# A recurrent-memory transformer block on one core: first rows ahead of the weights, one more key projection in the opening, one more feed-forward pair inside the recurrence

## The chip, the cores and the metric

The kernel runs on one core of a Trainium2 chip. The metric is the device time of one execution in microseconds (us); lower is better. The core has five engines with their own instruction streams: TensorE (PE) for matmuls, VectorE (DVE), ScalarE (ACT), GpSimd (POOL) and SyncE (SP), which only issues DMAs here. Each engine works through its own list in order.

## The reference

Two layers follow each other: attention over segments with a recurrent memory, then a gated feed-forward layer. Cut to what matters:

```python
# x: 2048 x 640, 32 heads of 128, segments of 32 tokens, memory of 8 rows
n_seg = 64; mem = mem0
for s in range(n_seg):
    h = concat([mem, LN(x)[32*s:32*s+32]])          # 40 rows
    q, k, v = h @ Wq, h @ Wk, h @ Wv                # 640 -> 32 heads x 128
    scores = q @ k.T * scale                        # per head, 40 x 40
    scores = where(mask, scores, -1e9)              # memory columns always, the rest causal
    o = (softmax(scores) @ v) @ Wo                  # 4096 -> 640
    mem = o[:8]; outs.append(o[8:])
h = x + concat(outs)
gate, up = LN(h) @ W_gate, LN(h) @ W_up             # 640 -> 1728
out = h + (relu(gate) * up) @ W_down                # 1728 -> 640
```

The memory makes the 64 segments a chain: segment s + 1 needs the first eight output rows of segment s.

## The kernel before

**Order of the work.** Every instruction is added to one list by hand (`add`), and `_Graph.solve` derives the waits from the keys that each names as read (`r`) or written (`w`). Within an engine the order of adding is the order of execution, so an instruction that waits holds up all that is behind it on its engine. A DMA that reads a tile holds the tile's next writer until it has landed. Most DMAs are issued by SP.

**Rows of a segment.** A segment has 40 rows: eight memory rows, 24 further rows ("early" tokens) and eight last ones ("late" tokens, `RID` = 24 to 31). A projection for a segment takes 32 columns at a time: memory and early tokens of that segment in `act_r`, and the late tokens of four segments together in `act_e`. `project` computes one of Wk, Wq, Wv (`j` = 1, 0, 2) for such a set of 32 rows: five chunks of the contraction, two halves of the heads, four matmuls of 128x512 side by side in column groups of 32, 40 matmuls in all.

**Opening.** The three attention weights come in 15 chunks of 1 MB in the order keys, queries, values, then Wo in eight pieces, all through SP. Meanwhile the first row sets are normalised (`row_stats`, `row_scale`, `ln1_trans`, `ln1_back`) and projected as each chunk lands (`opening`). `unit(n, j, ...)` projects the late tokens of later segments (`LATER[n]`), which need nothing of the memory: n = 0, 1, 2 are the groups of segments 58 to 61, 54 to 57 and 50 to 53. `keep` puts the keys and queries found into tiles that are idle in the opening (`HOMES`), and `spill` saves them to DRAM (`next_d`) when the opening is over. `warm` issues filler matmuls on a zeroed tile. The opening ends when segment 0's output has gone through Wo; its last product (`wo_pass`, L616) needs the last piece of Wo. Behind `spill` in SP's list come saves of the values in `Vp` (`lastv_d`), of `tok` 2 and 3 (`farv_d`) and of `ends`.

**Steps.** The loop `for s in range(1, 64)` runs a step per segment, some 12 us each: keys, queries and values of segment s, scores, softmax, values, Wo, and the memory for s + 1 (`to_act_split`). In step 1 the first half of the queries goes to `tok` 2. In the stretch where the recurrence leaves TensorE nothing to do, a step has an extra unit (`extra_units`): in the steps s % 4 = 2, 3, 0 the keys, queries and values of the late tokens of the next four segments; in s % 4 = 1 the Wo product of late tokens. In steps s of `EARLY` and the three after each, one block of 128 rows is finished, normalised and turned for the feed-forward layer (`xn2_d`). `fill_of` says how many projection matmuls of a step are cut into two halves of 256 columns.

**Pairs ahead of time.** Late tokens of the last segments have been projected in the opening, so the extra unit of steps 46 to 48, 50 to 52, 54 to 56 and 58 to 60 (`EARLY_STEPS`) is free and holds `early_product`: one pair (gate and up, 128 columns of the 1728) of the feed-forward layer for a block of 512 rows. Its rows and weights are fetched in the step before (`early_rows`, `early_weights`), its result goes to `hx_d`. There are nine pairs of block 0 (`NE`) and three of block 1 (`NX`).

**Feed-forward.** After the last segment come blocks 0 to 3 of 512 rows: 13 pairs and a tail each (`gate_up`, L1095 and L1108) less what was done ahead, then the down products (`down_pair`, L1434 and L1449). Block 1 loads the pairs done ahead from `hx_d` into `hT[1]`.

Of the kernel before, what the change touches and what calls it, by code (L numbers as in the profile page):

```python
# [177 lines left out]
def build_kernel(nc, A_x, A_mem0, A_Wq, A_Wk, A_Wv, A_Wo, A_seg_len, B_W_gate, B_W_up, B_W_down, out):  # L178
# [23 lines left out]
    NE = 9  # L202
    NX = 3
    next_d = [nc.dram_tensor(f"next{i}_d", [128, 32 * H], BF16) for i in range(6)]
# [73 lines left out]
    rs = ar.alloc("rs", [128, 1], F32)  # L278
    ps = es.enter_context(nc.psum_tensor("ps", [128, 4096], F32))
# [26 lines left out]
    add("pool", lambda p: p.memset(wtok[:], 0.0), w=[("wtok",)])  # L306
# [51 lines left out]
    def row_moments(src, skey, n, more=()):  # L358
        for q in range(2):
            add("dve", lambda v, q=q: v.bn_stats(st[0:n, q, :], src[0:n, q * 320:(q + 1) * 320]), r=[skey, *more],  # L360
                w=[("st", q)])
        add("dve", lambda v: v.bn_aggr(mv[0:n, :], st[0:n, :, :]), r=[("st", 0), ("st", 1)], w=[("mv",)])

    def row_std(n):
        add("act", lambda a: a.activation(lv[0:n, :], mv[0:n, 1:2], ACTF.Ln, bias=eps[0:n, 0:1], scale=1.0),
            r=[("mv",), ("eps",)], w=[("lv",)])
        add("act", lambda a: a.activation(rs[0:n, :], lv[0:n, :], ACTF.Exp, scale=-0.5), r=[("lv",)], w=[("rs",)])
# [5 lines left out]
    def row_scale(src, skey, n, dst, dkey, eng="dve"):  # L373
        add(eng, lambda v: v.tensor_scalar(dst[0:n, :], src[0:n, :], mv[0:n, 0:1], rs[0:n, 0:1], ALU.subtract,
                                             ALU.mult), r=[skey, ("mv",), ("rs",)], w=[dkey])
# [73 lines left out]
    HEAD = 64 + SEG + M  # L449
# [8 lines left out]
    def ln1_back(b, src, r, eng, kinds=(0, 1)):  # L458

        n = n_rows(b)  # L460

        def copy(dst, sl, w):
            if eng == "pool":
                add("pool", lambda p: p.tensor_copy(dst, sl), r=r, w=w)
            else:
                add("dve", lambda v: v.tensor_copy(dst, sl), r=r, w=w)
        if b < 0:
            copy(act_r[1][:, 0:2, :, M:32], src[:, :, 0:2 * SEG].rearrange("p c (e t) -> p e c t", t=SEG)[:, :, :, 0:RID],
                 [("act", 1, "x", e) for e in range(2)])
            for e, t0 in ((0, RID), (2, 2 * SEG)):  # L470
# [303 lines left out]
    def mem_load(g, eng):  # L774
        dma(wtok[32 * g:32 * g + M, :, :],
            mem0_ap.rearrange("t (c g j) -> g t c j", g=4, j=32)[g], r=[("wtok",)], w=[("wtok0", g)], eng=eng)

    for g in range(3):
        mem_load(g, "act")
    srcs = (A_Wq, A_Wk, A_Wv)  # L780
    for j in (1, 0, 2):
        for c in range(DC):
            dma(W[:, j, c, :], srcs[j][128 * c:128 * c + 128].rearrange("p h e -> p (h e)"), w=[("W", j, c)])
            if j == 1 and c == 0:
                mem_load(3, "sp")
            if j == 1 and c == 1:
                dma(xl[0:LATE, :], x_ap[SEG * (NSEG - 14):SEG * (NSEG - 2), :].rearrange("(e t) d -> e t d", t=SEG)[:, RID:SEG, :],
                    w=[("xl",)])
# [15 lines left out]

    warm(20)
    ln1_trans(-1, xt, ("xt",), P0)
    ln1_back(-1, chunks_of(bank_bf(P0)[:, 0:D]), [B(P0)], "dve")
# [6 lines left out]
    LATER = tuple((act_r[1][:, 4 - n], [("act", 1, 4 - n, "m"), ("act", 1, "x", 4 - n), ("act", 1, "x")]) for n in (1, 2)) + (  # L814
        (xl[:, 0:DC * 32].rearrange("p (c t) -> p c t", t=32), [("xl",)]),)
# [12 lines left out]
    opening(1, 0, (0, 1))  # L828
    warm(6)
    row_stats(x0, ("oTe", 0), 128)  # L830
    row_scale(x0, ("oTe", 0), 128, x0, ("oTe", 0))
    ln1_trans(0, x0, ("oTe", 0), P1)
    ln1_back(0, chunks_of(bank_bf(P1)[:, 0:D]), [B(P1)], "dve", (1,))
    opening(1, 0, (2,))
    warm(2)
    row_stats(xl, ("xl",), LATE)
    w0 = bank(P0)[:, 0:160]
    copy_op("dve", w0, wtok[:].rearrange("p c t -> p (c t)"), [("wtok",)] + [("wtok0", g) for g in range(4)],
            [B(P0), ("w0",)])
    to_act(0, ("w0",), w0)  # L840
    row_scale(xl, ("xl",), LATE, xl, ("xl",))
    ln1_back(0, chunks_of(bank_bf(P1)[:, 0:D]), [B(P1)], "dve", (0,))
    opening(1, 1, range(3))
    opening(1, 0, (3,))
    opening(1, 1, (3,))
    opening(1, 2, range(4))
# [3 lines left out]
            late_rows[:, :, 32:96].rearrange("p c (e t) -> p c e t", t=32), [B(P0)], LATER[0][1][:2] + LATER[1][1][:2])  # L850
    copy_op("dve", LATER[2][0], late_rows[:, :, 0:32], [B(P0)], [("xl",)])
# [3 lines left out]
    def turn(j, n, t):  # L855
        for i in range(2):
# [3 lines left out]
            else:  # L860
# [5 lines left out]
    HOMES = {(0, 1): [(Ve[0], 512 * i, VE_KEYS) for i in range(2)], (0, 0): [(oTe, 512 * i, oTe_keys) for i in range(2)],  # L866
             (1, 1): [(oT[1], 512 * i, OT_KEYS) for i in range(2)], (1, 0): [(at, 0, [("at",)]), (xt, 0, [("xt",)])],
             (2, 1): [(Ko, 512 * i, [("Ko", i) for i in range(2)]) for i in range(2)],
             (2, 0): [(Qo, 512 * i, QO_KEYS) for i in range(2)]}

    def keep(n, j, banks, t):
        for i in range(2):
            home, off, ks = HOMES[n, j][i]
            to_tok(banks[i], t + i, "act")
            add("dve", lambda v, home=home, off=off, i=i: v.transpose(ap(home, off, [[1, 512]]), tok[t + i][:, :]),
                r=tok_keys(t + i), w=ks)

    def spill(n, j):
        parts = HOMES[n, j]
        k = 2 * n + 1 - j  # L880
        if parts[0][0] is parts[1][0]:
            dma(next_d[k][:, :], ap(parts[0][0], 0, [[1, 32 * H]]), r=parts[0][2], w=[("next", k)])
            return
        for i, (home, off, ks) in enumerate(parts):
            dma(next_d[k][:, 512 * i:512 * i + 512], ap(home, off, [[1, 512]]), r=ks, w=[("next", k, i)])

    PP, TT = (P0, P1), (T0, T1)
    turn(1, 0, 0)
    turn(1, 1, 2)
    unit(0, 1, PP)  # L890
    turn(1, 2, 0)
# [3 lines left out]
    keep(0, 1, PP, 2)  # L895
    unit(1, 1, PP)
# [53 lines left out]
    def early_rows(s, lo, hi):  # L950
        q, b = 1 - place(s)[0], EARLY_STEPS.index(s) // NE
# [12 lines left out]
    def early_weights(s, q):  # L964
        t, k = early_tile(s, q)
        j = EARLY_STEPS.index(s) % NE
        dma(t[:, :], we_d[:, j, q, :], r=[("we_d", j, q)], w=[k])

    EARLY_STEPS = (NSEG - 18, NSEG - 17, NSEG - 16, NSEG - 14, NSEG - 13, NSEG - 12, NSEG - 10, NSEG - 9, NSEG - 8, NSEG - 6, NSEG - 5, NSEG - 4)

    def early_product(s):
        n, hp = EARLY_STEPS.index(s), 1 - place(s)[0]
# [66 lines left out]
    EARLY = tuple(range(11, 43, 4))  # L1039
# [98 lines left out]
    unit(1, 0, TT)  # L1138
# [3 lines left out]
    keep(1, 0, TT, 2)  # L1142
# [50 lines left out]
    spill(2, 0)  # L1193
    late_q(1)
# [15 lines left out]
    def fill_of(s):  # L1210
        n = {1: 0, 2: 5, 46: 0, 47: 25, 48: 40, 52: 40, 56: 40, 50: 0, 51: 25, 54: 0, 55: 25, 57: 39, 58: 0, 59: 27, 60: 40, 61: 39, 62: 50, 63: 0}.get(s, FILL[s % 4])
# [4 lines left out]
    for s in range(1, NSEG):  # L1216
# [16 lines left out]
        if s > 0:  # L1233
# [71 lines left out]
            if s == NSEG - 19:  # L1305
# [65 lines left out]
        late_q(s + 1, [("oT", par, "m", 1)])  # L1371
        if s in (NSEG - 16, NSEG - 12, NSEG - 8):
            early_rows(s + 2, 2, 4)
# [28 lines left out]
        if woe:  # L1402
            woe_sum(BQ[0])
            woe_store(s // 4 - 1)
            if s in (NSEG - 19, NSEG - 15, NSEG - 11, NSEG - 7):
# [212 lines left out]
```

## Time and profile before

| | |
|---|---|
| median of 3 runs | 970.49 us (969.31 to 971.04) |
| the profiled execution | 969.38 us |
| its span, first to last instruction | 967.7 us |
| mean granted TensorE clock | 0.999 |
| busy: TensorE, VectorE, ScalarE, GpSimd | 958.4, 726.4, 521.4, 186.0 us |
| read from and written to DRAM | 53.62 and 16.40 MB |

The profile is of one execution. A matmul's busy time includes the way through the array, so matmuls in a row overlap; the spacing of their starts is what TensorE needs for one. An idle time is given with the event that ended it. The chain that ended last is followed back from the last instruction.

### The profile page before, as it was taken

To read this page: it belongs to the slowest core of one execution; us is meant where nothing else is said; L and a number is where in the kernel's file an instruction comes from. 1 tells how busy PE (TensorE), PEld (TensorE's weight loads), DVE (VectorE), ACT (ScalarE), POOL (GpSimd) and SP (SyncE) were. 2 spreads that over 40 slices of the span, in tenths; PEclk is the share of its full clock that TensorE was granted. 3 is DMA by queue.
4 is the path that set the end of the run, shared out by engine and by line. 5 is a ranking of instruction groups with operands and counts; after the bars stand their busy time and mean duration, and the time that the engine had idled before them with its cause. 6 is when DMAs were issued, how large, how long until landed. Compare 5 with 4: busy or idle time off the path is not lost.

```text
span 967.7 us, 56757 instructions
## 1 busy us (share of the span) xinstructions
PE 958.4 (99%) x26193; PEld 532.9 (55%) x24889; DVE 726.4 (75%) x2044; ACT 521.4 (54%) x1324; POOL 186.0 (19%) x422
## 2 busy tenths in 40 slices
PE   8999999999999999999999999999999999999998
PEld 1245665556665656565556565666666666444443
DVE  5578888888888888888888888888878885355332
ACT  2466666666666666666666666565555563122120
POOL 7021111131323231313131302020201001000000
PEclk9999999999999999999999999999999999999999
DMA  9971222223232323232323223242425238823000
GB/s 362 415 265 54 44 49 43 70 50 79 51 81 57 81 57 81 61 79 59 85 62 77 63 42 92 71 123 78 128 70 127 70 90 263 296 33 98 28 7 28
DMA packets 100272, 96.00 MB, mean 99 GB/s; under 512 B 57926, under 2 KB 82734, under 8 KB 97966
## 3 DMA queue, kind: packets, MB, share of 16 engines
q1 hardware_dynamic: 98300, 91.41, 33.0%
q8 instruction: 201, 3.29, 1.5%
q10 hardware_dynamic: 1730, 0.96, 0.4%
q14 instruction: 41, 0.34, 0.1%
HBM read 53.62 MB, written 16.40 MB: 72 GB/s over the span
## 4 chain that ended last, share of the span: by engine, by line
PE 93%; SPq 3%; DMA 2%; DVE 1%; issue 0%; POOL 0%; ACT 0%; ACTq 0%; POOLq 0%
PE ps L418 46%; PE ps L1095 9%; PE ps L616 7%; PE ps L633 7%; PE ps L391 7%; PE ps L682 4%; SPq L356 3%; PE ps L1434 3%; PE ps L946 3%; PE ps L514 3%; PE ps L711 2%; DMA Wo<-in_A_Wo_dram 2%; PE ps L568 2%; PE ps L1108 0%; PE ps L1449 0%
## 5 line engine op out<-in xcount | busy, mean ns | idle before, releaser
L418 PE MATMUL ps<-W,act_r 128*32 128x512 bf16 (+1 forms) x8319 | 464.6, 359 | 0.2
L418 PEld LDWEIGHTS ps<-W,act_r 128*32 128x32 bf16 x8319 | 217.0, 96 | 166.0 <-issue 23.4
L442 ACT ACTIVATE tok<-ps 128x512 bf16<-128x512 f32 x184 | 106.2, 594 | 64.3 <-PE ps L418 45.8
L442 ACT ACTIVATE tox<-ps 128x512 bf16<-128x512 f32 x138 | 81.9, 599 | 61.9 <-PE ps L418 52.1
L437 DVE STREAM_TRANSPOSE Ko<-tox 128x512 bf16<-128x512 bf16 x128 | 89.1, 697 | 31.2 <-ACT tox L442 30.4
L596 DVE STREAM_TRANSPOSE oT<-tox 128x512 bf16<-128x512 bf16 x128 | 94.5, 739 | 0.0
L418 PE MATMUL ps<-W,act_e 128*32 128x512 bf16 x936 | 89.2, 379 | 2.4 <-DMA W<-in_A_Wv_dram 1.0
L437 DVE STREAM_TRANSPOSE Qo<-tok 128x512 bf16<-128x512 bf16 x126 | 86.8, 690 | 4.9 <-ACT tok L442 4.1
L616 PE MATMUL ps<-Wo,oT 128*32 128x160 bf16 x4032 | 81.7, 233 | 0.5 <-DMA Wo<-in_A_Wo_dram 0.5
L633 PE MATMUL ps<-Wo,oT 128*32 128x320 bf16 x2016 | 79.9, 299 | 0.0
L616 PEld LDWEIGHTS ps<-Wo,oT 128*32 128x32 bf16 x4032 | 70.5, 97 | 10.7 <-DVE oT L590 3.1
L442 ACT ACTIVATE Vp<-ps 128x512 bf16<-128x512 f32 x127 | 75.1, 592 | 0.5 <-ACT Vp L442 0.5
L649 ACT ACTIVATE SA<-TA 64x40 f32<-64x40 f32 x126 | 29.6, 235 | 65.1 <-DVE TA L646 64.3
L391 PE MATMUL ps<-W,act_e 128*32 128x512 bf16 x664 | 64.6, 379 | 0.0
L530 ACT ACTIVATE Pm<-ps 128x64 bf16<-128x64 f32 x126 | 28.2, 224 | 65.9 <-PE ps L514 63.5
L590 DVE STREAM_TRANSPOSE oT<-om 128x128 bf16<-128x128 bf16 x126 | 39.1, 311 | 31.5 <-ACT om L582 31.4
L1123 ACT ACTIVATE g<-ps 128x512 bf16<-128x512 f32 x40 | 23.2, 594 | 72.4 <-PE ps L1095 72.4
L514 PE MATMUL ps<-Qo,Ko 128*32 128x40 bf16 x2048 | 61.1, 181 | 0.1
L514 PEld LDWEIGHTS ps<-Qo,Ko 128*32 128x32 bf16 x2048 | 46.4, 94 | 26.3 <-DVE Qo L437 18.7
L633 PEld LDWEIGHTS ps<-Wo,oT 128*32 128x32 bf16 x2016 | 50.9, 96 | 17.6 <-issue 0.8
L522 POOL COPY Qo<-ends 128x256 bf16<-128x256 bf16 x32 | 14.0, 438 | 230.0 <-DVE oT L590 207.4
L522 POOL COPY Qo<-Qe 128x256 bf16<-128x256 bf16 x32 | 14.1, 440 | 229.0 <-DVE oT L590 229.0
(164 smaller groups left out, 1573.5 us busy)
## 6 DMA issues: line engine op xcount, KB each, us to landing
VM<-Vp SPq DMA_DIRECT2D x126, 65.0 KB
VM<-Vp SPq DMA_DIRECT2D x63, 130.0 KB
W<-in_A_Wk_dram SPq DMA_DIRECT2D x5, 1024.0 KB
W<-in_A_Wq_dram SPq DMA_DIRECT2D x5, 1024.0 KB
W<-in_A_Wv_dram SPq DMA_DIRECT2D x5, 1024.0 KB
Wo<-in_A_Wo_dram SPq DMA_DIRECT2D x8, 640.0 KB
attn_d<-wtok SPq DMA_DIRECT2D x248, 7.5 KB
xt<-in_A_x_dram SPq DMA_DIRECT2D x16, 160.0 KB
```

The source lines that it names most:

```text
L391: return pe.add_instruction(mybir.InstMatmult(name=nc.get_next_instruction_name(), engine=mybir.EngineType.PE, ins=[pe.lower_ap(rhs), pe.l ...
L418: ins = pe.matmul(*b, start=(c == ends[0]), stop=(c == ends[1]), skip_group_check=True)
L437: add("dve", lambda v: v.transpose(dst[:, 16 * i:16 * i + 16, 0:32], tok[t][:, :].rearrange("p (h f) -> p h f", f=32)), r=tok_keys(t), w=keys)
L442: add("act", lambda a: a.activation(dst, src, ACTF.Copy), r=r, w=w)
L514: i = pe.matmul(bank((P0, P1)[hf])[q:q + 32, o:o + 40], (Ko if a == 0 else Ke[p])[:, h, :], Qo[:, h, :], start=True, stop=True, skip_group ...
L590: add("dve", lambda v: v.transpose(ap(oT[par], 160 * hf, [[40, 4], [320, 4], [1, 8]]), ap(om, 128 * hf, [[1, 4], [4, 32]])), r=[("om", hf) ...
L596: add("dve", lambda v, kh=kh: v.transpose(ap(oT[p], 160 * kh + M, [[320, 4], [40, 4], [1, 32]]), ap(tox, 128 * kh, [[256, 4], [1, 4], [4, ...
L616: i = pe.matmul(bank(bk)[32 * gg:32 * gg + 32, 0:160], src[:, hb, 0:32], w[:, gg], start=(hb == CH[16 * halves[0]]), stop=(hb == CH[-1]), ...
L633: i = pe.matmul(bank(bk)[32 * q:32 * q + 32, 0:320], src[:, hb, 0:32], w, start=(n == 0), stop=(n == 7), skip_group_check=True)
L649: add("act", lambda a, lo=lo, to=to: a.activation(SA[to:to + 64], TA[lo:lo + 64, 1, :, 0:M], ACTF.Copy), r=[("TA", 1)], w=[("SA", to)])
L682: ins = pe.matmul(bank(bk)[32 * q:32 * q + 32, 0:320], src[:, hb, 0:32], w[:, 2 * (q % 2):2 * (q % 2) + 2], start=(i == 0), stop=(i == 15) ...
L1095: ins = pe.matmul(bank(bk), w[:, c, lo:lo + 128], xn2T[par][:, c, :], start=(c == 0), stop=(c == DC - 1))
```

## The change

1. The first rows: one DMA of 128 rows (64 from each end of the input) as SP's first, ahead of the first chunk of Wk. Before, two DMAs of 64 and 40 rows went through ScalarE's queue. The next 128 rows, the memory rows and the late rows go through ScalarE's queue. The statistics of the first two row sets have tiles of their own (`SETS`).
2. The memory rows are loaded as eight rows and turned by TensorE (`transpose_rows(at, ...)`), in place of four DMAs of 32-column pieces and a transpose on VectorE.
3. The opening gets the late rows of segments 46 to 49 too (`LATE` = 128 rows) and their keys: `unit(3, 1, TT)`. It takes the place of `unit(1, 0, TT)`, which moves to the end of the query phase; the order of units, copies and fillers (`warm`, 28 before, 17 after) is new. The keys are kept in six scraps of tiles and saved by six DMAs (`spill(3, 1)`), placed between the save of `Qo` and that of `oTe`; they are read back at step 43.
4. Step 42, whose extra unit had those keys, holds the fourth pair of block 1 (`NX` = 4). Its loads are issued in step 41. For this the rows of the feed-forward layer are prepared four steps earlier (`EARLY` starts at 7). Block 1 has nine pairs left.
5. `fill_of` has new entries for steps 3, 4, 42 and 43.

```diff
-    NX = 3
+    NX = 4
...
-    for p0, p1, t0, key in ((0, 64, 0, ("xt",)), (64, HEAD, S - HEAD + 64, ("xt", "late"))):
-        dma(xt[p0:p1, :], x_ap[t0:t0 + p1 - p0, :], w=[key], eng="act")
+    dma(xt[:, :], bass.AP(x_ap.tensor, x_ap.offset, [[(S - 64) * D, 2], [D, 64], [1, D]]), w=[("xt",)])
     ln1_load(0, x0, ("oTe", 0), "act")
-    LATE = 3 * 4 * M
...
-    for g in range(3):
-        mem_load(g, "act")
+    dma(at[0:M, :], mem0_ap, w=[("at",)], eng="act")
+    LATE = 4 * 4 * M
+    dma(xl[0:LATE, :], x_ap[SEG * (NSEG - 18):SEG * (NSEG - 2), :].rearrange("(e t) d -> e t d", t=SEG)[:, RID:SEG, :],
+        w=[("xl",)], eng="act")
...
-    row_stats(xt, ("xt",), HEAD, [("xt", "late")])
+    row_halves(xt, ("xt",), HEAD)
+    row_join(HEAD)
+    row_std(HEAD)
+    row_halves(x0, ("oTe", 0), 128, k=1)
     row_scale(xt, ("xt",), HEAD, xt, ("xt",))
+    row_join(128, 1)
+    row_std(128, 1)
...
-    warm(20)
+    warm(8)
     ln1_trans(-1, xt, ("xt",), P0)
+    warm(2)
...
+             (3, 1): [(0, Qo, 1024, 256, QO_KEYS), (256, oT[1], 1024, 256, OT_KEYS), (512, at, 512, 128, [("at",)]),
+                      (640, xt, 512, 128, [("xt",)]), (768, wtok, 0, 160, [("wtok",)]), (928, ident, 0, 96, [("ident",)])]}
...
-    unit(0, 0, PP, range(4))
-    for n in (2, 0, 1):
+        unit(0, 0, PP, ((0, 1, 2), (3,))[c - 2])
+    unit(0, 0, PP, (4,))
+    for n in (1, 2, 0):
         opening(0, n, (4,))
-    unit(0, 0, PP, (4,))
-    for n, t in ((2, 2), (0, 0), (1, 2)):
+    keep(0, 0, PP, 0)
+    for n, t in ((1, 2), (2, 0), (0, 2)):
         turn(0, n, t)
     late_q(0)
-    keep(0, 0, PP, 0)
+    unit(1, 0, PP)
+    keep(1, 0, PP, 0)
...
-    EARLY_STEPS = (NSEG - 18, NSEG - 17, ...
+    EARLY_STEPS = (NSEG - 22, NSEG - 18, NSEG - 17, ...
...
-    EARLY = tuple(range(11, 43, 4))
+    EARLY = tuple(range(7, 39, 4))
...
     first_values((0, 1))
-    unit(1, 0, TT)
+    unit(3, 1, TT)
     scores(0, 0)
     scores(0, 1)
     first_values((2,))
-    keep(1, 0, TT, 2)
+    keep(3, 1, TT, 2)
...
     spill(2, 0)
+    spill(3, 1)
     late_q(1)
     spill(0, 0)
...
-        n = {1: 0, 2: 5, 46: 0, ...
+        n = {1: 0, 2: 5, 3: 0, 4: 48, 42: 0, 43: 41, 46: 0, ...
...
+            elif s == NSEG - 21:
+                dma(ends[:, 0:32 * H], next_d[6][:, :], r=[("next", 6, i) for i in range(6)], w=END_KEYS[0:2])
```

More of the change, by code (lines that the diff above doesn't have):

```diff
@@ L202, in build_kernel @@
     NE = 9
-    NX = 3
-    next_d = [nc.dram_tensor(f"next{i}_d", [128, 32 * H], BF16) for i in range(6)]
+    NX = 4
+    next_d = [nc.dram_tensor(f"next{i}_d", [128, 32 * H], BF16) for i in range(7)]
     nextv_d = nc.dram_tensor("nextv_d", [128, 8 * VW], BF16)
@@ L826, in unit @@
             project(a, ks, j, (0, 1), banks, (c,), late=True)
[L828 to L831, printed above, removed]
+    opening(1, 0, (0,))
+    warm(4)
+    row_scale(x0, ("oTe", 0), 128, x0, ("oTe", 0), k=1)
     ln1_trans(0, x0, ("oTe", 0), P1)
     ln1_back(0, chunks_of(bank_bf(P1)[:, 0:D]), [B(P1)], "dve", (1,))
-    opening(1, 0, (2,))
-    warm(2)
+    transpose_rows(at, ("at",), M, P0)
+    copy_op("dve", act_r[1][:, 0, :, 0:M], chunks_of(bank_bf(P0)[:, 0:D])[:, :, 0:M], [B(P0)],
+            [("act", 1, 0, "m"), ("act", 1, 0, "m2")])
+    opening(1, 1, (0,))
+    warm(3)
     row_stats(xl, ("xl",), LATE)
[L837 to L840, printed above, removed]
+    ln1_back(0, chunks_of(bank_bf(P1)[:, 0:D]), [B(P1)], "dve", (0,))
     row_scale(xl, ("xl",), LATE, xl, ("xl",))
[L842 to L846, printed above, removed]
+    opening(1, 0, (1,))
+    opening(1, 1, (1,))
+    opening(1, 2, (0, 1))
     transpose_rows(xl, ("xl",), LATE, P0)
@@ L849, in build_kernel @@
     copy_op("dve", act_r[1][:, 2:4].rearrange("p e c t -> p c e t"),
-            late_rows[:, :, 32:96].rearrange("p c (e t) -> p c e t", t=32), [B(P0)], LATER[0][1][:2] + LATER[1][1][:2])
-    copy_op("dve", LATER[2][0], late_rows[:, :, 0:32], [B(P0)], [("xl",)])
+            late_rows[:, :, 64:128].rearrange("p c (e t) -> p c e t", t=32), [B(P0)], LATER[0][1][:2] + LATER[1][1][:2])
+    copy_op("dve", xl[:, 0:2 * DC * 32].rearrange("p (e c t) -> p c e t", e=2, t=32),
+            late_rows[:, :, 0:64].rearrange("p c (e t) -> p c e t", t=32), [B(P0)], [("xl",)])
+    for n in range(3):
+        opening(1, n, (2,))
+    unit(0, 1, (P0, P1), range(3))
+    for n in range(3):
+        opening(1, n, (3,))
+    unit(0, 1, (P0, P1), (3, 4))
     for n in range(3):
@@ L880, in spill @@
         k = 2 * n + 1 - j
[L881 to L882 removed]
+        if parts[0][1] is parts[1][1]:
+            dma(next_d[k][:, :], ap(parts[0][1], 0, [[1, 32 * H]]), r=parts[0][4], w=[("next", k)])
             return
[L884 to L885 removed]
+        for i, (lo, home, off, w, ks) in enumerate(parts):
+            dma(next_d[k][:, lo:lo + w], ap(home, off, [[1, w]]), r=ks, w=[("next", k, i)])
     PP, TT = (P0, P1), (T0, T1)
[L888 to L891, printed above, removed]
+    keep(0, 1, PP, 0)
+    for n, t in ((0, 2), (1, 0), (2, 2)):
+        turn(1, n, t)
+    unit(1, 1, PP)
     for c in range(2):
```

81 lines of the change are left out of this document (44 added, 37 removed).

## The prediction

> **What bounds the kernel now.** I read the page's busy times and chain shares first, then the chain in order of time, then the opening engine by engine.
>
> ```profile
> PE 958.4 (99%) x26193; PEld 532.9 (55%) x24889; DVE 726.4 (75%) x2044; ACT 521.4 (54%) x1324; POOL 186.0 (19%) x422
> PE 93%; SPq 3%; DMA 2%; DVE 1%; issue 0%; POOL 0%; ACT 0%; ACTq 0%; POOLq 0%
> ```
>
> The first line is the busy time of each engine, the second the share of each in the chain that ended last. TensorE holds 93% of that chain. What is not TensorE lies at the start, as the chain in order of time says (start, length, what):
>
> ```profile
> 36.14 20.26 DMA Wo<-in_A_Wo_dram
> 56.41 0.04 issue
> 56.45 0.46 PE ps L616 x16
> ...
> 838.36 21.58 PE ps L1095 x100
> 859.95 1.09 PE ps L1108 x10
> ```
>
> So there are two regimes. Up to 56.4 us the weights arrive, and the last piece of Wo sets the end of the opening. After that TensorE runs without a break. Work taken out of the second regime is gained in full; work put into the first is free as long as it fits into the holes that TensorE has there.
>
> **The pair that leaves block 1.** L1095 is the gate and up products. Block 1 makes ten pairs in 21.58 us, 100 matmuls back to back, 2.16 us a pair. The change takes pair 3 out: **-2.16 us**. The load of finished pairs grows from three to four (128 KB); it is wanted only by the down products, after 19 us of other gate and up work, so it is hidden. Without that cover it would cost what 128 KB takes at the 398 GB/s shown further down, 0.3 us.
>
> **The same pair in step 42.** There it takes the place of the projection of the late keys of segments 46 to 49. Both are 40 matmuls, by these groups of the same shape (count, busy us, mean ns):
>
> ```profile
> L418 PE MATMUL ps<-W,act_e 128*32 128x512 bf16 x936 | 89.2, 379 | 2.4 <-DMA W<-in_A_Wv_dram 1.0 <-DVE act_e L466 0.8 <-DMA W<-in_A_Wk_dram 0.2
> L946 PE MATMUL ps<-ends,xt 128*32 128x512 bf16 x120 | 7.5, 379 | 0.0
> ...
> 595.00:607.00 12.00, 12.00 (x386) 7.01 (x367) 10.40 (x33) 7.36 (x20) 5.35 (x11) 1.00 0.36 103
> ```
>
> Zero on TensorE. Steps 41 to 43 put seven more DMAs into SP's queue (two weights, three pieces of rows, the store, the saved keys read back), ahead of the merged values of the next step. The last row is the stretch in which steps 45 and 46 already do the same: TensorE is busy 12.00 of 12 us (columns PE, PEld, DVE, ACT, POOL). Between 0 and 0.2 us, I take **+0.1**. If a merge came late, TensorE would wait for it at the start of a step. The rows of blocks 0 and 1 are prepared one round of four steps earlier, which moves POOL's and SP's work from steps 39 to 42 to steps 7 to 10 and changes no amount: 0, at most 0.2 either way. The regrouped halves in steps 3, 4, 42 and 43 stream the same columns: 0.
>
> **One more projection in the opening.** It is ten groups of four matmuls, one each 0.215 us in the rows below (34.03 to 34.24): 2.15 us. A pass, one of its five chunks, is two such groups, 0.43 us. TensorE's own rows, where it stood still in the opening (start, length, last bracket the releaser):
>
> ```profile
> 23.41 0.39 PE L391 MATMUL ps<-W,act_r 128*32 128x512 bf16 x4
> 24.00 0.40 PE L418 MATMUL ps<-W,act_e 128*32 128x512 bf16 x4 [0.20 <-DMA W<-in_A_Wq_dram]
> ...
> 33.51 0.39 PE L391 MATMUL ps<-W,act_r 128*32 128x512 bf16 x4
> 34.03 0.40 PE L418 MATMUL ps<-W,act_e 128*32 128x512 bf16 x4
> 34.24 0.40 PE L391 MATMUL ps<-W,act_e 128*32 128x512 bf16 x4
> 34.76 0.40 PE L418 MATMUL ps<-W,act_r 128*32 128x512 bf16 x4
> 34.99 0.39 PE L391 MATMUL ps<-W,act_r 128*32 128x512 bf16 x4
> 36.42 0.40 PE L418 MATMUL ps<-W,act_e 128*32 128x512 bf16 x4 [1.04 <-DMA W<-in_A_Wv_dram]
> ...
> 55.58 0.39 PE L391 MATMUL ps<-W,act_r 128*32 128x512 bf16 x4
> 56.45 0.46 PE L616 MATMUL ps<-Wo,oT 128*32 128x160 bf16 x16 [0.48 <-DMA Wo<-in_A_Wo_dram]
> ```
>
> Starts beyond a spacing of 0.215 us are holes: 0.37, 0.30, 0.30 and 1.21, together 2.2 us up to 36.42, and 0.65 before the last Wo. The change fills the earlier holes: the last key projection of the value phase moves to the end of the query phase, the new one takes its place, so the value phase keeps its length. 2.15 into 2.2 just fits, and the start helps:
>
> ```profile
> 6.39 0.89 DVE L360 BATCH_NORM_STATS2 st<-xt 104x6 f32<-104x320 bf16 x2 [4.80 <-DMA xt<-in_A_x_dram]
> 9.86 0.40 PE L418 MATMUL ps<-W,act_e 128*32 128x512 bf16 x4 [0.78 <-DVE act_e L466]
> ...
> 5.00:10.00 5.00, 4.22 (x22) 0.40 (x9) 2.13 (x7) 0.50 (x2) 3.76 (x19) 1.00 1.02 354
> 10.00:15.00 5.00, 4.30 (x47) 0.89 (x23) 3.10 (x11) 0.50 (x2) 3.78 (x18) 1.00 1.01 412
> ```
>
> The first rows land at 6.39 and the first key pass starts 3.47 us later. With the rows ahead of the first chunk they land some 3 us earlier; VectorE then does the statistics of the next rows before it scales the first, so I count on 1.1 us of it, an estimate. Spare is then 2.2 + 1.1 - 2.15 = 1.15 us ahead of the value phase. One thing takes from the end: the first value passes overwrite the banks of the last query passes, and ScalarE must now empty four pairs of banks (1.09 us a pair, the row ACT 47.12 below) after the last query chunk, 4.4 us, while TensorE has three passes, the moved projection and one value pass, 1.3 + 2.15 + 0.4 = 3.9 us. That is 0.5 us late against a hole of 0.65: **0**, and 0.2 us from costing. If the cover is gone, each us late is a us lost.
>
> **The saves behind Wo.** The new keys wait in six scraps of tiles and go out as six DMAs, between the save of Qo and the others, 256 KB in 768 rows of 192 to 512 bytes. Step 1 waits for one of the saves behind them:
>
> ```profile
> 47.12 1.08 ACT L442 ACTIVATE tok<-ps 128x512 bf16<-128x512 f32 x2 [0.64 <-PE ps L391]
> ...
> 61.77 0.60 ACT L442 ACTIVATE tok<-ps 128x512 bf16<-128x512 f32 x1 [0.63 <-DMA farv_d<-tok]
> 62.40 0.71 DVE L437 STREAM_TRANSPOSE Qo<-tok 128x512 bf16<-128x512 bf16 x1 [0.25 <-ACT tok L442]
> 63.26 0.20 PE L514 MATMUL ps<-Qo,Ko 128*32 128x40 bf16 x4
> ...
> DMA packets 1205, 1.99 MB, mean 398 GB/s; under 512 B 134, under 2 KB 685, under 8 KB 1204
> q1 hardware_dynamic: 1204, 1.97, 105.0%
> ...
> q1 hardware_dynamic: 4465, 2.47, 25.6%
> ```
>
> ScalarE may not write tok before its old content has been saved (farv). Queued behind that copy are VectorE's transpose of the queries and TensorE's scores, which start at 63.26, 0.15 us after the transpose ends at 63.11. That is all the slack, and nothing stands behind the scores on TensorE that it could take first. What do the six DMAs cost? No row has them. From below: 256 KB at 398 GB/s (the DMA view, 57 to 62 us), 0.64 us. From above: that view has 69.8 ns for a packet of 1636 bytes (105% of 16 engines over 5 us), the same view over 300 to 340 us, the last row, 36.7 ns for 553 bytes; the line through both gives 30 ns at 341 bytes, and 768 of them on 16 engines 1.45 us. I take 1.0. All of this moves with the weight stream, whose rate is 354 GB/s between 5 and 10 us and 412 after: if the rows ahead of it mend that, it ends 0.7 us sooner; the 80 KB more of rows make it 0.2 later. I take 0.1 sooner. So scores of step 1 come 1.0 - 0.1 - 0.15 = **+0.75 us** late, between 0 and 1.5, and TensorE has no hole afterwards in which to win it back.
>
> **Sum.** -2.16 + 0.1 + 0 + 0.75 = -1.3 us. The profiled execution took 969.38 us (span 967.7 and 1.7 around it), so it would become 968.1; the median of the runs is 970.49, 1.11 above the profiled one, which gives **969.2 us**. A difference under 0.2%, 1.9 us, is about what a measurement of this kernel can't tell from none; the forecast lies inside.
>
> **Rivals.** *The saves cost nothing.* The weight stream ends 0.7 us sooner and the scraps take 0.64: the copy of step 1 comes when it came, steps 41 to 43 cost nothing, and the full 2.16 stays: 968.3 us. For it: the low rate between 5 and 10 us, where row loads and weights mix. Against: an opening bound by bytes gets more bytes.
>
> *The opening runs at half clock: slower.* The filler matmuls at the start show two speeds (count, busy us, mean ns, 1.6 to 7.1 us and 7.1 to 8.6 us):
>
> ```profile
> L391 PE MATMUL ps<-oT 128*128 128x512 bf16 x12 | 5.3, 630 | 0.0
> ...
> L391 PE MATMUL ps<-oT 128*128 128x512 bf16 x8 | 2.1, 405 | 0.0
> ```
>
> Twelve take 5.3 us, 0.44 each, the next eight 2.1. Before, 20 run until the first transposes. After, 8 end at about 5.2 us (they start when the zeroed tile is there, at 1.65), the rows are ready no sooner than 7, and TensorE stands still between. If it then stays slow, each key pass costs 0.43 us more. Cover is 1.15 ahead of the value phase and 0.15 at its end; from there up to 0.75 the loss hides behind the wait for the saves, and 1.3 more eats what the sum gained. It decides from 3.35 us on, eight passes; with fifteen passes slow (all that the keys of the opening's three row sets need) the loss is 6.45 us, 3.1 beyond that point: 970.49 + 3.1 = 973.6 us. Against it: with passes and fillers TensorE is busy nearly without a break from about 8 us on. [...]
>
> **How the numbers follow.** The forecast 0.44, the saves for nothing 0.38, the half clock 0.18. By its bounds the first runs from -2.16 to -2.16 + 0.3 + 1.5 = -0.36 us, 968.3 to 970.1, nearly all of it within 0.2% (above 968.55); the second is faster by more, the third slower, mostly by more. Faster 0.38, same 0.46, slower 0.16. The range for 8 in 10 runs from 967.8, the second case less half a us (the three runs lie up to 1.2 from their median, 969.31 to 971.04), to 971.5, the third with ten slow passes: it leaves out most of the third.
>
> **What would show it.** Right: block 1's gate and up line has 90 matmuls in 19.4 us; the last Wo pass starts within half a us of 56.45; in step 1 ScalarE's copy waits for farv, and the scores start 0.75 us later after that Wo pass than the 6.81 us of before; steps 41 to 43 are as long as their neighbours. Wrong: TensorE comes late to the last Wo piece (no DMA wait there); matmuls of 0.43 us spacing after 10 us; or the scores of step 1 on time.

## The result: 4.4 us slower

| | median | runs |
|---|---|---|
| kernel before | 970.76 us (969.31 to 971.91) | 6 |
| changed kernel | 975.14 us (973.60 to 976.86) | 6 |

The ratio is 1.0045, with a 95% interval from 1.0032 to 1.0059: slower by 3.1 to 5.7 us. The prediction was 969.2 us, with a range up to 971.5. The profiled execution took 974.78 us (span 973.0, granted clock 1.0), 5.4 us more than that of before.

### The profile page after: what moved, and what is told of

Its sections match the earlier page's. It is cut to its first block, busy times and chain, and to the rows that moved or that the text cites. A ratio compares the mean times of both kernels' runs of the same rounds, so it can differ in the third digit from the quotient of the medians.

```text
span 973.0 us, 56745 instructions
## 1 busy us (share of the span) xinstructions
PE 959.2 (99%) x26186; PEld 534.5 (55%) x24874; DVE 725.8 (75%) x2047; ACT 520.7 (54%) x1324; POOL 185.4 (19%) x421
## 4 chain that ended last, share of the span: by engine, by line
PE 97%; DVE 1%; DMA 1%; ACT 1%; issue 0%
PE ps L430 48%; PE ps L403 9%; PE ps L1117 8%; PE ps L628 7%; PE ps L645 7%; PE ps L694 4%; PE ps L963 3%; PE ps L1461 3%; PE ps L526 3%; PE ps L723 2%; PE ps L580 1%; DMA xt<-in_A_x_dram 1%; PE ps L1130 0%; ACT tok L454 0%; PE ps L1476 0%
```

## The profile after

The chain that ended last, in order of time (start, length, what):

```profile
0.80 7.53 DMA xt<-in_A_x_dram
...
829.45 0.92 issue
...
845.41 19.43 PE ps L1117 x90
864.84 1.09 PE ps L1130 x10
```

Block 1 is as predicted: 90 matmuls in 19.43 us for 100 in 21.58. What is new stands at the top. Before, the chain of the opening was one wait for Wo until 56.41. Now it begins with 7.53 us of waiting for the first rows, and from there to the end of the opening it runs mostly through TensorE. The engines' rows (start, length, last bracket the idle time before and what ended it):

```profile
8.35 0.89 DVE L363 BATCH_NORM_STATS2 st<-xt 128x6 f32<-128x320 bf16 x2 [6.75 <-DMA xt<-in_A_x_dram]
10.63 0.71 PE L396 MATMUL ps<-ident,xt 128*128 128x128 bf16 x5 [5.39 <-DVE xt L386]
12.13 0.62 PE L430 MATMUL ps<-W,act_e 128*32 128x512 bf16 x4
16.44 0.62 PE L430 MATMUL ps<-W,act_e 128*32 128x512 bf16 x4 [0.69 <-DVE act_e L478]
18.81 0.62 PE L430 MATMUL ps<-W,act_e 128*32 128x512 bf16 x4
21.69 0.40 PE L430 MATMUL ps<-W,act_e 128*32 128x512 bf16 x4
...
61.85 0.45 PE L628 MATMUL ps<-Wo,oT 128*32 128x160 bf16 x16
65.26 0.42 PE L723 MATMUL ps<-VM,Px 64*32 64x129 bf16 x32
67.36 0.60 ACT L454 ACTIVATE tok<-ps 128x512 bf16<-128x512 f32 x1 [0.83 <-DMA farv_d<-tok]
67.99 0.71 DVE L449 STREAM_TRANSPOSE Qo<-tok 128x512 bf16<-128x512 bf16 x1 [0.45 <-ACT tok L454]
68.85 0.20 PE L526 MATMUL ps<-Qo,Ko 128*32 128x40 bf16 x4
```

The rows come at 8.35, not some 3 us before the old 6.39 but 2 us behind it. TensorE stands still for 5.39 us, and the first key pass starts at 12.13 for 9.86. Then matmuls of 0.62 us for 0.40. By the starts, the two halves of a pass lie 0.40 to 0.43 us apart for 0.22 before: half rate, until 20 us. TensorE comes to the last Wo pass at 61.85 with no DMA wait, 5.40 after the 56.45 of before.

In what follows, the first and second pass over VM (matmuls that every step has once; L723, L711 in the kernel before) are the marks: one stands at the end of the opening, the other a step later. Before, they start at 59.87 and 72.01, after at 65.26 and 77.88. So the opening costs 5.39 us and step 1 another 0.47. The rest of the profile goes: steps 2 to 60 +0.79 (two single steps, 15 and 57, are 12.46 and 12.34 long), from there to block 0's down products +0.4 (the 0.92 us of "issue" above are 0.22 before), block 1 -2.15, the end +0.5; together the 5.4 us between the two profiled executions.

## Experiments

Four sets (e1 to e4, e5 to e8, e9 and e10, e11 and e12); each has its own runs of the kernel before (medians 971.38, 970.78, 971.22 and 971.07 us). The last two columns are the two marks in the profile of each.

| run | median, us | ratio to before | mark 1 | mark 2 |
|---|---|---|---|---|
| before | | 1 | 59.87 | 72.01 |
| the change | 975.14 | 1.0045 [1.0032, 1.0059] | 65.26 | 77.88 |
| e1 rows_two_dmas | 973.54 | 1.0014 [1.0004, 1.0025] | 61.50 | 75.79 |
| e2 rows_alone | 974.74 | 1.0032 [1.0020, 1.0043] | 63.51 | 75.57 |
| e3 more_fillers | 975.98 | 1.0048 [1.0036, 1.0059] | 63.21 | 79.29 |
| e4 saves_reordered | 971.79 | 1.0006 [0.9995, 1.0016] | 60.89 | 74.43 |
| e5 saves_by_need | 971.54 | 1.0003 [0.9992, 1.0013] | 61.84 | 75.51 |
| e6 by_need_fillers | 972.02 | 1.0010 [0.9999, 1.0021] | 61.59 | 76.44 |
| e7 rows_two_alone | 971.93 | 1.0013 [1.0005, 1.0022] | 61.19 | 73.23 |
| e8 six_more_saves | 972.46 | 1.0021 [1.0012, 1.0030] | 59.93 | 73.86 |
| e9 order2_fillers | 972.22 | 1.0010 [1.0000, 1.0021] | 60.86 | 75.16 |
| e10 order2 | 970.86 | 0.9994 [0.9985, 1.0002] | 59.85 | 73.86 |
| e11 far_by_act | 970.59 | 0.9992 [0.9983, 1.0001] | 60.59 | 72.79 |
| e12 far_by_act_before | 971.68 | 1.0005 [0.9996, 1.0015] | 60.81 | 74.32 |

A profile is one execution, and the runs of one kernel lie up to 5.6 us apart (e4: 969.99 to 975.59), so a mark of one profile is read with the row that explains it. The ratios lie nearer to the means of the runs than to the medians: e1 is 2.2 us above the kernel before by the medians, 1.4 by the ratio.

### The first rows: e2, e1, e7

The trace of after says more about the load of the first rows. Its 128 packets of 1280 bytes run from 2.5 to 7.5 us, and their durations sum to 10.3 us: by an estimate from these two numbers the work of two DMA engines, one packet behind the other. The semaphore that tells of its landing is counted up (a "post") once at 1.93, when nothing has landed, and then twice, at 8.16 and 8.32; the load of x0 is posted sixteen times between 2.83 and 3.15. The posts at the landing of the other row loads in the traces of before and after: sixteen for 64 and for 128 rows, twelve for the late rows of before (12 times 8), ten for 40 rows, eight for eight; where they are fewer than sixteen, one more comes early (at 2.53 us for the 40 rows). The source pattern here is [2][64][640], and the two posts at the landing go with its outermost 2. So I take it that this load ran on two engines; the traces don't say which engine carries a packet. What lies behind it comes late by two posts too. Of the sixteen posts of the first chunk of Wk, fourteen come by 7.69 and the last two at 11.41 and 11.53; of the last piece of Wo, fourteen by 57.11 and the last two at 58.72 and 58.76. Before, that piece has landed at 56.41.

e2 puts only this load into the kernel before (the number of rows, `HEAD`, and one offset follow it):

```diff
-    for p0, p1, t0, key in ((0, 64, 0, ("xt",)), (64, HEAD, S - HEAD + 64, ("xt", "late"))):
-        dma(xt[p0:p1, :], x_ap[t0:t0 + p1 - p0, :], w=[key], eng="act")
+    dma(xt[:, :], bass.AP(x_ap.tensor, x_ap.offset, [[(S - 64) * D, 2], [D, 64], [1, D]]), w=[("xt",)])
```

> The kernel before with only the load of its first rows taken from the change: one DMA with an outer dimension of two, first in SP's queue, 128 rows instead of 104; 20 fillers as before, no further projection, no further pair. Theory (two engines): the rows land at about 8.3 us, Wk's first chunk at about 11.5, the last piece of Wo at about 58.8 instead of 56.4, and as the opening ends with it, the whole is 2.4 us slower than before, 973.2 us (972.5 to 975). Rival 1 (clock): with 20 fillers the array is warm when the first pass comes, so before's 970.8. Rival 2 (one projection too many): no further projection here, so 970.8.

It took 3.2 per mille more, 1.9 to 4.2 us: the load alone makes most of the loss. TensorE waits for the last piece of Wo, which lands at 60.05, 3.64 later than before; mark 1 is later by the same 3.64:

```profile
60.09 0.46 PE L616 MATMUL ps<-Wo,oT 128*32 128x160 bf16 x16 [0.86 <-DMA Wo<-in_A_Wo_dram]
```

e1 leaves the change as it is but for this load:

```diff
-    dma(xt[:, :], bass.AP(x_ap.tensor, x_ap.offset, [[(S - 64) * D, 2], [D, 64], [1, D]]), w=[("xt",)])
+    for p0, t0, key in ((0, 0, ("xt",)), (64, S - 64, ("xt", "late"))):
+        dma(xt[p0:p0 + 64, :], x_ap[t0:t0 + 64, :], w=[key])
```

> The changed kernel with its first rows as two DMAs of 64 rows (one from each end of the input) in place of one DMA with an outer dimension of two; still first in SP's queue. Theory (the one DMA of the changed kernel runs as two rows of packets side by side, lands at 8.3 us and holds up those two engines' share of every weight chunk behind it): the first rows land at about 3 us, the first chunk of Wk near 6 (11.5 in the changed kernel), the last piece of Wo near 56.6 (58.8), the first key pass starts at 7 to 9 (12.1), and the whole takes 969.5 us, 968.5 to 971. Rival 1 (clock: only 8 filler matmuls, TensorE falls to half rate and stays there): the key passes still have spacings of 0.43 us until 14 to 20 us, and 2 to 3 us of the loss remain, 972.5. Rival 2 (the opening simply has one projection too many for TensorE): the last Wo pass still starts near 61, 974 to 975.

It wins back 3 of the 4.4 us by the ratios (2.2 by the medians), not all: 969.5 was expected. The last piece of Wo lands at 56.47, as in the kernel before, but TensorE comes to it only at 57.96, after matmuls at half rate until 16.3 us. That is rival 1. e7 is e2 with the load cut in two in the same way:

> The kernel before with only the first rows moved ahead of the first weight chunk on SP's queue, as two DMAs of 64 rows. Theory (what cost 3.4 us in the run rows_alone was that one DMA ran on two of the 16 engines): no cost, 971.2 us, within 0.5 of the kernel before. Rival (any row load ahead of the first chunk puts the whole row of weights back): 973 or more.

The rows that waited for the first rows in e2 and in e7, and TensorE's next wait in e7:

```profile
8.27 0.89 DVE L360 BATCH_NORM_STATS2 st<-xt 128x6 f32<-128x320 bf16 x2 [6.68 <-DMA xt<-in_A_x_dram]
```
```profile
4.88 0.89 DVE L360 BATCH_NORM_STATS2 st<-xt 128x6 f32<-128x320 bf16 x2 [3.29 <-DMA xt<-in_A_x_dram]
11.91 0.41 PE L418 MATMUL ps<-W,act_e 128*32 128x512 bf16 x4 [2.28 <-DMA W<-in_A_Wk_dram]
```

Two DMAs of 64 rows bring the rows 3.4 us earlier than one of 128. The theory for e7 was half right: by the ratios 1.9 of e2's 3.1 us are gone, but 1.3 (0.5 to 2.1) stay. SP comes to the first chunk of weights 1.28 us later (2.07 for 0.79); the second lands at 11.87 us, before at 10.25, and TensorE waits 2.28 us for it; the last piece of Wo lands at 57.73 for 56.41. These 1.3 us aren't the price of any two loads in front: e1 has the same two, and its last piece lands at 56.47. Between 5 and 10 us its DMAs move 420 GB/s, those of e7 345. e1 also has the change's other loads of memory and late rows; no run separates these.

### Half clock: e3

The second loss that the rows show is the half rate until 20 us. e3 fills the hole ahead of the first rows:

```diff
-    warm(8)
+    warm(28)
```

> The changed kernel with 28 fillers at the start in place of 8, so that TensorE has something to do until the first rows are turned at about 10.6 us; the rows' DMA stays as in the change. Theory (two engines set the start, the half clock is a second part): the fillers pass to spacings of 0.22 us at about 7 us, the key passes run at 0.22 from the first one on, the last Wo pass starts when the last piece of Wo lands, 58.8, instead of 61.85: some 3 us of the 4.4 come back, 972.3 us. Rival 1 (clock alone): all of the loss comes back, 969.5 to 970.5. Rival 2 (one projection too many): 974 to 975.

The groups of the first projections between 8 and 24 us, in after and in e3 (count, busy us, mean ns), then e3's rows at the end of the opening:

```profile
L430 PE MATMUL ps<-W,act_e 128*32 128x512 bf16 x24 | 3.3, 538 | 0.7 <-DVE act_e L478 0.7
```
```profile
L430 PE MATMUL ps<-W,act_e 128*32 128x512 bf16 x40 | 3.9, 383 | 1.1 <-DVE act_e L478 1.1
```
```profile
63.21 0.42 PE L723 MATMUL ps<-VM,Px 64*32 64x129 bf16 x32
67.64 0.60 ACT L454 ACTIVATE tok<-ps 128x512 bf16<-128x512 f32 x1 [3.15 <-DMA farv_d<-tok]
69.13 0.20 PE L526 MATMUL ps<-Qo,Ko 128*32 128x40 bf16 x4 [2.36 <-DVE Qo L449]
71.85 0.67 PE L430 MATMUL ps<-W,act_r 128*32 128x512 bf16 x4
```

The fillers did what they should: full rate, a wait for the last piece of Wo again (0.37 us), and the opening ends 2.05 us earlier, at 63.21. The time didn't move. ScalarE's copy to `tok` comes at 67.64, where it came at 67.36 in after: its wait for the save of the far values grew from 0.83 to 3.15. Two chains end the opening, one close behind the other, and e3 shortened one of them.

The second one isn't held by the place in SP's queue. SP sent that save 1.36 us earlier in e3 (the first row) than in after (the second):

```profile
63.59 0.94 SPq L356 DMA_DIRECT2D farv_d<-tok  x2
```
```profile
64.95 0.94 SPq L356 DMA_DIRECT2D farv_d<-tok  x2
```

Fifteen of its sixteen posts are there at 65.93, and the last comes at 67.55 (after: 67.21 and 67.28). So here one late post holds the copy, not the place in the queue. TensorE stands still for 2.36 us, and from 69.76 to 72.73 most matmuls of 512 columns take 0.59 to 0.63 us each for 0.38 (the row above is a group of four): half rate once more, so step 1 takes 16.08 us for 12.62. This profile is of e3's slowest run (978.45 us); it shows what can eat the gain, not what did in each run.

### The saves behind the opening: e4, e5, e8

SP's queue in the kernel before, and in e1 (start, time on the queue, what; a time above 0.5 for a single one holds a wait):

```profile
53.23 1.35 SPq L356 DMA_DIRECT2D next_d<-xt  x1
54.62 1.30 SPq L356 DMA_DIRECT2D lastv_d<-Vp  x1
56.63 1.66 SPq L356 DMA_DIRECT2D farv_d<-tok  x2
```
```profile
53.18 1.56 SPq L356 DMA_DIRECT2D next_d<-Qo  x2
54.78 1.25 SPq L356 DMA_DIRECT2D next_d<-oT  x1
56.07 1.16 SPq L356 DMA_DIRECT2D next_d<-at  x1
57.27 0.44 SPq L356 DMA_DIRECT2D next_d<-xt  x1
57.74 0.44 SPq L356 DMA_DIRECT2D next_d<-wtok  x1
58.22 0.43 SPq L356 DMA_DIRECT2D next_d<-ident  x1
58.70 0.43 SPq L356 DMA_DIRECT2D next_d<-oTe  x1
...
60.67 1.45 SPq L356 DMA_DIRECT2D lastv_d<-Vp  x1
62.17 0.92 SPq L356 DMA_DIRECT2D farv_d<-tok  x2
```

In e1 and in after a save of this stretch that waits for nothing still holds the queue for 0.43 to 0.50 us, from start to start 0.48. Before, the queue stood ready for the far values, which are in `tok` at 57.1. In e1 they go out at 62.17, 2.9 us after they are there (59.26). e1's step 1:

```profile
64.99 0.60 ACT L454 ACTIVATE tok<-ps 128x512 bf16<-128x512 f32 x1 [2.22 <-DMA farv_d<-tok]
66.48 0.20 PE L526 MATMUL ps<-Qo,Ko 128*32 128x40 bf16 x4 [1.43 <-DVE Qo L449]
```

That is the wait that the prediction had at +0.75 us. With the opening 1.63 us late in place of 5.39 the scores stand 4.98 us behind the first mark for 3.39, 1.59 later, and step 1 takes 14.29 us for 12.15. In the changed kernel the late opening hid most of it. e8 measures it by itself: six more saves of these sizes in the kernel before, nothing else.

```diff
     spill(2, 0)
+    for lo, home, off, w, ks in ((0, Qo, 0, 256, QO_KEYS), (256, oT[1], 0, 256, OT_KEYS), (512, at, 0, 128, [("at",)]),
+                                 (640, xt, 0, 128, [("xt",)]), (768, Qo, 256, 160, QO_KEYS), (928, Qo, 416, 96, QO_KEYS)):
+        dma(more_d[:, lo:lo + w], ap(home, off, [[1, w]]), r=ks, w=[("more", lo)])
```

> The kernel before with six more saves, of the sizes of the change's scrap saves (256 KB in all), behind the same save as there, into memory that nothing reads: nothing else is changed. Theory (a place in SP's queue costs 0.43 to 0.50 us, six of them 2.8; 0.7 of it fits into the queue's wait for the far values): step 1 is 2.1 us longer, time 973.4. Rival (only the bytes count: 256 KB at some 410 GB/s are 0.6 us): 972.0 at most.

```profile
63.67 0.60 ACT L443 ACTIVATE tok<-ps 128x512 bf16<-128x512 f32 x1 [2.47 <-DMA farv_d<-tok]
```

2.1 per mille, 2.0 us (1.2 to 2.9), and step 1 at 13.93: near the 2.1 us of the places in the queue, beyond the 0.6 us of the bytes. But the sum behind the 2.1 isn't shown. The six saves land 0.18 to 0.21 us apart, 1.14 in all, so by packets they cost the DMA engines more than by bytes. SP comes to the far values 4.18 us later (60.81 for 56.63), not 2.1 or 2.8, and holds 1.6 us at the save of Vp. Fifteen of their sixteen posts come by 62.83, the last at 63.59; before, all sixteen by 61.69. How much of the 2.0 us is the queue and how much the engines stays open. e4 moves the two far saves forward, to behind the save of Qo and its scrap:

```diff
-    spill(3, 1)
+    spill(3, 1, (0,))
     late_q(1)
+    for i in range(2):
+        dma(farv_d[:, 512 * i:512 * i + 512], tok[2 + i], r=tok_keys(2 + i), w=[("farv", i)])
     spill(0, 0)
     spill(1, 1)
+    spill(3, 1, (1, 2, 3, 4, 5))
     spill(1, 0)
```

> The kernel with the rows as two DMAs, and the saves behind the opening in another order: the two saves of tok that step 1 waits for go right behind the saves of Qo (256 KB and one scrap of 64 KB), ahead of those of oTe, oT, the five other scraps, at, xt and Vp. Theory: in step 1 the copy of the first half of the queries no longer waits for a DMA, the scores start 6.8 us after the last Wo pass as in the kernel before (7.4 to 7.6 without this edit), 0.6 to 0.9 us faster than the kernel with the two DMAs alone: 968.7. Rival (the wait in step 1 is hidden by the late opening): no difference.

e5 puts the save of Vp and the other scraps ahead of them, while the queue waits for the far values anyway:

```diff
     spill(3, 1, (0,))
+    dma(lastv_d[:, :], ...)
     late_q(1)
+    spill(3, 1, (1, 2, 3, 4, 5))
     for i in range(2):
         dma(farv_d[...], tok[2 + i], ...)
     spill(0, 0)
     spill(1, 1)
-    spill(3, 1, (1, 2, 3, 4, 5))
     spill(1, 0)
```

> The changed kernel with its first rows loaded by two DMAs of 64 rows, and the saves behind the opening in another order on SP's queue: the save of Vp and five of the six scrap saves go while the queue would wait for the far values, then the two saves of the far values, then the other saves. Theory (six more saves take 0.43 to 0.50 us of SP's queue each, and step 1's wait for the far values is the end of that queue): the wait of 2.22 us goes, and so does the 1.67 us on the save of Vp that the earlier order had; step 1 falls from 14.29 us to about 12.2, time 971.4 us, beside 971.4 for the kernel before. Rival (the bytes of the saves on the DMA engines, not the places in the queue, are what the far values wait for): over 1 us of the wait is left, time 972.5.

Each order takes one wait away and shows the next, here in e4 and in e5:

```profile
66.83 0.60 ACT L454 ACTIVATE Vp<-ps 128x512 bf16<-128x512 f32 x1 [1.67 <-DMA lastv_d<-Vp]
```
```profile
66.56 0.71 DVE L608 STREAM_TRANSPOSE oT<-tox 128x512 bf16<-128x512 bf16 x1 [1.40 <-issue]
```

In e4 the save of Vp is late. In e5 VectorE waits to write the odd `oT`, whose save (SP at 62.09) landed at 66.48; the row says "issue", and only the landing time names the cause. Fifteen of the sixteen posts of that save were there at 64.45, so it was one late post again. By the ratios both gain about a us on e1. For e4 0.6 to 0.9 was expected, but from an e1 at 969.5; for e5 2.1, and its step 1 takes 13.67 us where 12.2 was expected. Neither is told from the kernel before.

### Both together: e6, e9, e10, e11, e12

e6 is e5 with more fillers at the four places ahead of and between the first passes:

```diff
-    warm(8)
+    warm(11)
...
-    warm(2)
+    warm(6)
...
-    warm(4)
+    warm(6)
...
-    warm(3)
+    warm(4)
```

> The kernel of the run saves_by_need with more filler matmuls ahead of and between the first passes (11, 6, 6 and 4 for 8, 2, 4 and 3). Theory (with the rows loaded in time it is the half clock, from the hole at 5.2 us to 16 us, that puts the opening 1.6 us behind the last piece of Wo): all passes from 8.8 us on at 0.22 us, the first pass over VM at 59.9 us for 61.5, time 969.8 us, 1.5 below the kernel before. Rival (fillers gave nothing in the changed kernel as it is, so PE isn't what ends the opening): 971.4, as without them.

e10 is e5 with the save of the odd `oT` ahead of SP's wait for the next rows (`ln1_load`), and e9 is e10 with e6's fillers:

```diff
     spill(2, 1)
+    spill(1, 1)
     ln1_load(1, xl, ("xl",))
     spill(2, 0)
-    spill(3, 1, (0,))
+    spill(3, 1, (0, 1))
     dma(lastv_d[:, :], ...)
     late_q(1)
-    spill(3, 1, (1, 2, 3, 4, 5))
+    spill(3, 1, (2, 3, 4, 5))
...
-    spill(1, 1)
```

> The kernel of the run by_need_fillers with the saves once more in another order: the save of the odd O^T rows, whose values are there 5 us before SP's wait for the next segment's rows, goes ahead of that wait, and the scrap save that lies behind it in the same tile goes second. In saves_by_need that save landed at 66.48 us and held DVE's write into the tile, and with it step 1, until 66.56. Theory (three chains end the opening one behind the other: the passes, the save of the far values, the saves of O^T and Vp; with all three in time step 1 takes 12.2 us behind a first pass over VM at 60.2): the block's 2.15 us are left over, less 0.6 elsewhere, time 969.4 us where the kernel before takes 970.8. Rival (PE's stall of 2.4 us with nothing to wait for in by_need_fillers comes back, since a 16 KB packet of the instruction queue that came every 4 to 5 us before comes after 7.2 behind the saves): step 1 at 14 us or more in the profile, time 971.5.

> The same order of saves without the added fillers (8, 2, 4 and 3 as in the change). Theory: the first pass over VM stays at 61.6 us, by the half clock until 16 us, and step 1 takes 12.2 us; time 971.0. Rival (the clock in the opening doesn't matter, only the saves do): 969.4, like the run with the fillers.

Here the theory fell for the fillers. e6 isn't faster than e5, nor e9 than e10; by the medians both are slower, by 0.5 and 1.4 us. e9's row shows what its rival had named:

```profile
68.92 0.39 PE L430 MATMUL ps<-W,act_r 128*32 128x512 bf16 x1 [1.61 <-issue]
```

TensorE stood for 1.61 us in the middle of step 1 with nothing to wait for; in e6 for 1.89, at 69.92. Shorter stands of this kind end the opening: 0.90 us in e6 (at 57.75; its first mark is at 61.59 where 59.9 was expected), 0.60 in e9, and 0.70 in e5 without the fillers (at 58.43). The instruction queue's 16 KB packets come every 4 to 5 us; in e9 one starts at 59.36 and the next at 66.46, in e6 at 60.20 and 67.43, and TensorE goes on 1.5 to 1.6 us after the late one has ended in both. Before, they start at 59.43, 64.42 and 67.91, and there is no such stand. That TensorE waited for its own instructions behind the saves fits, but no run was made to show it. Against it, e8 has packets as far apart (59.08 and 66.40) and no such stand; why it comes in step 1 of the two runs with more fillers is open.

e10 is level with the kernel before: 0.9994 [0.9985, 1.0002]. Its first mark is at 59.85, with a DMA wait at the last Wo piece again, and with no more fillers than the change:

```profile
56.44 0.46 PE L628 MATMUL ps<-Wo,oT 128*32 128x160 bf16 x16 [0.29 <-DMA Wo<-in_A_Wo_dram]
```

Both halves of its theory missed: the mark was expected at 61.6 and came early, since full rate was there from 12.3 us on in this execution; step 1 was expected at 12.2 us and took 14.01. That the time came out near the 971.0 forecast is luck. The last two runs move the two far saves from SP's queue to ScalarE's, in e10 (e11) and in the kernel before (e12):

```diff
-        dma(farv_d[...], tok[2 + i], r=tok_keys(2 + i), w=[("farv", i)])
+        dma(farv_d[...], tok[2 + i], r=tok_keys(2 + i), w=[("farv", i)], eng="act")
```

> The kernel of the run order2 with its two saves of the far values issued on ScalarE's queue, right behind the evacuations that fill them, and not behind the other saves on SP's. Theory (the far values wait in SP's queue behind saves that nothing needs so early): ScalarE's wait of 1.09 us for that save goes, for 0.4 us an issue on ScalarE, step 1 13.3 us for 14.01, time 970.2 us beside 971.0 for the kernel before. Rival (the 16 engines have the bytes of all saves to move whichever queue holds them): the wait stays, and ScalarE's two issues come on top, 971.5.

> The kernel before with the same one edit: its two saves of the far values on ScalarE's queue. Theory: its wait of 0.63 us goes for 0.4 us an issue beside ScalarE's wait of 0.72 us for the next pass: 0.3 us less, 970.7 us where the kernel before takes 971.0. Rival (as in the other kernel): the wait stays and ScalarE is 0.5 us later, 971.5.

The far values in e10, and then in e11:

```profile
58.79 1.72 SPq L356 DMA_DIRECT2D farv_d<-tok  x2
62.22 0.60 ACT L454 ACTIVATE tok<-ps 128x512 bf16<-128x512 f32 x1 [1.09 <-DMA farv_d<-tok]
```
```profile
57.02 1.23 ACTq L356 DMA_DIRECT2D farv_d<-tok  x2
62.26 0.60 ACT L454 ACTIVATE tok<-ps 128x512 bf16<-128x512 f32 x1 [0.39 <-PE ps L430]
```

In e11 the wait is gone and step 1 takes 12.20 us, but ScalarE is 0.7 us later to the opening's last copies, and the time is that of e10 within its error: 0.9992 [0.9983, 1.0001]. In e12 nothing is gained:

```profile
57.12 1.56 ACTq L356 DMA_DIRECT2D farv_d<-tok  x2
63.81 0.60 ACT L442 ACTIVATE tok<-ps 128x512 bf16<-128x512 f32 x1 [1.72 <-DMA farv_d<-tok]
```

The saves go out about as early as before (57.12 for 56.63), but the first lands at 63.72 for 61.69, as all DMAs ahead of it end later in this execution (the last piece of Wo 0.94, the save of Vp 1.48). Here the rival held: the wait stays, whichever queue holds the save. e11 is the fastest of all by its median, 0.5 us below the kernel before, which these runs can't tell from no difference.

## Why the prediction was wrong

**What failed: the opening's 0.** The step is "With the rows ahead of the first chunk they land some 3 us earlier". It took the load's place in the queue for its time and didn't ask how the one DMA is cut over the engines. The rows came 2 us later, the first key pass 2.27 later, and the weights ended 2.35 us later where the prediction had 0.1 sooner. With that the sum of holes (2.2 + 1.1 - 2.15) had nothing left, and the term 0 measured +5.39: 2.35 for the weights, and the rest because TensorE, which began 2.27 us late and ran at half rate until 20 us, came to the last Wo pass 3.09 us after the last piece had landed. e2 and e1 show that this load makes about 3 us of the 4.4.

**What was mis-sized: the saves.** The mechanism is as predicted: ScalarE's copy waits for the far values, VectorE's transpose and the scores behind it. The price, 0.64 to 1.45 us by bytes and packets, left out the queue: six places of 0.48 us each on SP are 2.9. Alone (e8) it cost 2.0 us by time (1.2 to 2.9, which doesn't rule out 1.45), and the scores came 1.84 later behind the first mark; in e1 they came 1.59 later. In the changed kernel the scores stood 7.00 us after the last Wo pass for 6.81, and step 1 was 0.47 longer. That this is near the +0.75 of the sum is luck: the late opening hid the rest.

**The rival of half clock** was right in its mechanism: spacings of 0.43 us were there until 20 us. But e3 took them away and gained nothing, as the save of the far values ended step 1's wait no earlier, and with the rows in time the kernels at full rate (e6, e9) weren't faster than those without the fillers (e5, e10; the profile of e10 was at full rate from 12.3 us by itself). So what the half rate costs in time isn't shown.

**What held.** Block 1: -2.16 predicted, -2.15 measured. Steps 41 to 43, with the pair: 35.95 us for 35.90, +0.1 predicted. With the load and the order of saves mended (e10, e11) the time is 0.4 to 0.5 us below the kernel before; the prediction's sum of -1.3 us lies inside both intervals (-1.5 to +0.2, -1.7 to +0.1), near their lower ends; no difference lies inside them too.

## What to carry to other kernels

Before a DMA is merged from two, look at the outermost dimension of its pattern: here one that only counts two pieces landed 3.4 us later than two loads of 64 rows (e2 and e7); in after it had two posts at its landing, and of the first weights behind it two posts of sixteen came 3.7 us after the others. Price a small DMA by its place in the issuing queue as well as by its bytes (six saves here: 2.9 us of queue, 0.64 of bytes), and order saves by the time at which their tile is written next. Before a late save is put down to its place in the queue, look at its posts: in e3 and e5 fifteen of sixteen were there 1.6 and 2.0 us ahead of the last. Where two chains end a stage close behind one another, an experiment that shortens one can show nothing until the other is shortened too.

## What was unexpected of the hardware

**The rate differs between executions of the same matmuls.** e1, e4, e5, e10 and e11 have the same list of instructions on TensorE. The first projection pass from which full spacing (0.22 us) stayed began at 16.3 us in e1, 15.8 in e5, 12.6 in e11, 12.3 in e10 and 11.8 in e4. The records' granted clock doesn't tell: it is 1.00 in after between 10 and 20 us, where the spacing is 0.43. In e5 the first transposes, at 6.36 us, ran at full rate already (0.45 us for the five, 0.71 in after), TensorE then stood for 1.38 us, and from 9.26 on the spacing was 0.40 again. What lets the rate fall isn't shown: in e5 the holes between matmuls ahead of the fall were of 1.11 and 1.38 us, and in e3 the rate fell after one of 2.36.

**A wait can be hidden under "issue".** VectorE's 1.40 us in e5 ended 0.08 us after a save of the tile that it writes had landed, TensorE's 1.61 us in e9 1.5 us behind a late packet of the instruction queue. Neither row names its cause.

**One post of sixteen can come far behind the others.** The save of `oT` in e1 had fifteen posts at 61.51 and the last at 63.22, that of e5 at 64.45 and 66.48, the far values of e3 at 65.93 and 67.55. A packet of the instruction queue, 16 KB and 0.95 to 1.14 us long, starts 0.1 to 0.7 us ahead of each fifteenth post (60.80, 64.40, 65.22). That it held one DMA engine fits; the traces don't say which engine carries a packet.
